# Four edits at the ends of a 2D-FFT filter stage in a mixer kernel: order of a scale, an fp32 operand, copies between SBUF tiles, late weight splits

## The chip, the cores and the metric

The kernel runs on one core of one Trainium2 chip. The metric is the device time of one execution in microseconds (us). The time before is 972.05 us, the median of three runs that lie between 971.56 and 975.56 us.

## The reference

Two blocks A (a spectral filter) and B (a token MLP) alternate, twice each, on x of 2048 tokens by 640 channels:

```python
def _A_ref(x, w_r, w_i):
    X = rfft2(x)                 # over tokens and channels
    return irfft2(X * (w_r + 1j * w_i), (S, D))
def _B_ref(x, w1, b1, w2, b2):
    u = gelu(einsum("bsd,sf->bdf", layernorm(x), w1) + b1)
    return (einsum("bdf,fs->bds", u, w2) + b2).transpose(0, 2, 1)
x = x + _A_ref(layernorm(x), w_r, w_i)
x = x + _B_ref(layernorm(x), w1, b1, w2, b2)
x = x + _A_ref(layernorm(x), w_r, w_i)
x = x + _B_ref(layernorm(x), w1, b1, w2, b2)
```

## The kernel before

The filter block is done with matrix products against tables. Three stages of code carry it. In the first (`run` for block one, the last rows of `b1st` for block three) each of 16 token tiles is normalised, folded and multiplied by `tM`; the result goes to two tiles of fp16, the rounded value `s1h` and the remainder `s1l`, 80 columns of 128 values each: columns 0 to 63 are four classes of 16 groups, columns 64 to 79 one "rest" column for each group. Nearly every operand of the kernel is such a pair of fp16 values, and a product takes three fp16 matmuls.

The second stage is `a1`, called the filter stage here. It runs twice, in block one (about 60 to 121 us) and in block three (about 533 to 600 us). It goes over 16 groups g of frequencies. For each group there are these steps, in the names that the order string `STEPS` gives them:

- `d` (`dstage`): the products of `s1h`, `s1l` with the table `tD`, into a PSUM slot. Groups 0 and 1 read the rest column in place; groups from 2 on read it from a stacked tile `stk`, in which the parts of one group's rest column lie under each other on partitions 0 to 31, 32 to 63 and 64 to 95. `stack(g)` fills it for two groups at a time (three buffers).
- `ph`, `pl` (`psplit`): ScalarE writes the rounded value of that PSUM slot, scaled, to fp16, and VectorE the remainder. For group 0 this is written out ahead of the order string, in two halves q.
- `sA`, `sB` (`s2half`): two half products with the table `tS2`, each in four quarters of the array (64 rows by 64 columns), three fp16 terms each, 12 matmuls of 321 columns. The two halves add into the same banks, so each `sB` waits for an instruction that itself waited for `sA`. For group 0 this instruction is a small VectorE copy on a tile called `between`.
- `ta`, `tb` (`term`): VectorE multiplies with the filter `w` and its scale `sx`. `sa`, `sb`: GpSimd adds and subtracts the terms. `xh`, `xl` split the sum (ScalarE, GpSimd), `uh`, `ul` copy a strip (ScalarE).
- `i` (`is2mm`): the product with `tI2`. `Yh`, `Yl`: its split into the tile Y (ScalarE, VectorE).

`STEPS` holds one order for each of the two calls, and each engine runs its part of it in that order (`self.pin = True`). `d1@1` means group 1 in PSUM slot 1, `ph2&1` that this instruction stands between `sA1` and `sB1`. In the first call further steps beginning with `e` are mixed in: `ep8 ev8 ep9 ev9 ev10` are the pieces of `scale_x`, which works out the scale `sx` of the filter from the sums of squares `xq`, on TensorE (p) and VectorE (v), by way of a PSUM tile (slot 1); its last piece `ev10` gives `cxe`, which scales the input of the third stage. `ea4` to `ea7` are ScalarE's part of the split of a weight tile for block two (`wsplit` with `lo=False`, into `wh`), `ev4` the scale for it.

The rest columns go from `s1h`, `s1l` to DRAM tiles `rest` (`keep`, on SyncE's queue) and from there to `stk`, in `stack`: three DMAs for the three parts and two small ones for a single row. For groups 2 and 3 (`G0`) the parts from `s1h` are issued by GpSimd, all others by SyncE. GpSimd's memset of `between` comes after `stack(G0)` in the program. DMAs issued before the order string are placed by the scheduler of the framework.

The third stage is `a2`, over 16 token tiles i: `id_mm(i)` (16 matmuls with `tDi`), `ehigh` on ScalarE (`eh`, needs `cxe`), `elow` on VectorE (`el`), then `is1_mm` (6 matmuls with `tIM`) one tile later, then sums and statistics. VectorE's part of the split of that weight tile is in the loop, at tiles 1, 2, 4 and 5. The MLP blocks `b1st` and `b2nd` follow.

In `run`, over i from 0 to 21, ScalarE writes `s1h` and VectorE `s1l` of tile i - 6, VectorE the fold `f` of tile i - 4, and ScalarE sums the squares of one filter group per step (`scan_x`).

Of the kernel before, what the change touches and what calls it, by code (L numbers as in the profile page):

```python
# [11 lines left out]
F32 = mybir.dt.float32  # L12
# [15 lines left out]
    d1@1 ep8 ph1 sA0@0 ev8 pl1 sB0 ep9 sA1@1 ev9 d2@2 tb0 d3@3 ta0 ph2&1 pl2 sb0 sB1 sa0 ea1 sA2@2 tb1 ph3 d4@0 xh0&2  # L28
# [10 lines left out]
    Yh14 Yl12 xl15b i15a@0 uh15 ul15 Yl14 i15b@3 Yh15a Yh15b Yl15a Yl15b ev4 ev10 ea4 ea5 ea6 ea7  # L39
# [9 lines left out]
    sB14 pl15 sa13 i9@1 xh12 ta14 ul10 sb13 uh12 i8@3 Yh7 tb14 xl12 Yh9 sb14 sA15@0 xh13 sa14 Yl9 uh13 ul12&15 xl13  # L49
    xh14 sB15 Yl7 ul11 i10@1 uh14 Yh8 ta15a xl14 i11@2 tb15a Yh10 ta15b ul13 sa15a tb15b ul14 Yl8 Yh11 i13@0 sb15a  # L50
# [9 lines left out]
TS = 4096.0  # L60
# [30 lines left out]
class Layers:  # L91
# [226 lines left out]
    def a0_open(self, first=False):  # L318
# [5 lines left out]
        self.tS2 = p.tile([128, 2, 2, 4, 128], F16, name=f"tS2{self.n}")  # L324
        self.tI2 = p.tile([128, 2, 2, 2, 128], F16, name=f"tI2{self.n}")
        p = self.pT = self.push("a0", side=self.sp)
# [9 lines left out]
    def a0_load(self):  # L336
        nc, A = self.nc, self.A
        nc.sync.dma_start(self.tD, A["tD"])
        nc.sync.dma_start(self.tS2, A["tS2"])
        nc.sync.dma_start(self.tI2, A["tI2"])  # L340

# [126 lines left out]
    def a1(self, first):  # L468
# [35 lines left out]

        CL = [(1, 0, 0, 160, 96), (0, 0, 160, 321, 98), (3, 1, 0, 160, 96), (2, 1, 160, 321, 96)]
# [3 lines left out]
        def stack(g):  # L509
# [4 lines left out]
            r, c = rest[g > G0], slice(g - 4, g - 4 + NC) if g > G0 else slice(0, NC)  # L514
            for k, a in ((0, 0), (1, 1), (2, 0)):
                e = nc.gpsimd if g == G0 and not a else nc.sync
                e.dma_start(q[32 * k:32 * k + 32], r[a][:, :, c].rearrange("c i g r -> i c g r"))
                if k < 2:
                    e.dma_start(q[96 + k:97 + k, 0], r[k][2, 31:32, c])

        rest = [[self.dram.tile([4, 32, n, 128], F16, name=f"rest{i}_{n}_{self.n}") for i in range(2)] for n in (NC, NG - 4)]
        def keep(i, c):

            for q, s1 in zip(rest[i], (self.s1h, self.s1l)):
                nc.sync.dma_start(q.rearrange("c i g r -> (c i) g r"), s1[:, c].rearrange("p g h a b -> p g (h a b)"))

        keep(0, slice(66, 68))
        stack(G0)
        keep(1, slice(68, 80))
# [1654 lines left out]
```

## Time and profile before

| what | us |
|---|---|
| median of three runs | 972.05 |
| the profiled execution, whole | 976.39 |
| its span, first to last instruction | 974.6 |
| filter stage of block one, first to last matmul of its order | about 60.8 to 120.3 |
| filter stage of block three | about 533.2 to 597.7 |
| granted TensorE clock, mean | 0.995 |

A row of the timeline gives the start in us from the beginning of the span, the duration, the engine, the line, the operation, output and inputs by the program's names with their shape, the number of instructions merged into the row, and in brackets how long the engine sat idle before it and what released it. A row of the windows gives the length of a stretch, the busy time and number of instructions of PE (matmuls), PEld (weight loads), VectorE (DVE), ScalarE (ACT) and GpSimd (POOL), the granted TensorE clock as a share of full speed, the share of the DMA engines that was busy, and GB/s. SPq is SyncE's queue, on which DMAs are issued. Nearly all instructions carry line 83, that of a helper, so rows are told apart by their tiles.

### The profile page before, as it was taken

To read this page: it belongs to the slowest core of one execution; us is meant where nothing else is said; L and a number is where in the kernel's file an instruction comes from. 1 tells how busy PE (TensorE), PEld (TensorE's weight loads), DVE (VectorE), ACT (ScalarE), POOL (GpSimd) and SP (SyncE) were. 2 spreads that over 40 slices of the span, in tenths; PEclk is the share of its full clock that TensorE was granted. 3 is DMA by queue.
4 is the path that set the end of the run, shared out by engine and by line. 5 is a ranking of instruction groups with operands and counts; after the bars stand their busy time and mean duration, and the time that the engine had idled before them with its cause. 6 is when DMAs were issued, how large, how long until landed. Compare 5 with 4: busy or idle time off the path is not lost.

```text
span 974.6 us, 22438 instructions
## 1 busy us (share of the span) xinstructions
PE 933.2 (96%) x8993; PEld 694.1 (71%) x8993; DVE 752.1 (77%) x1403; ACT 564.8 (58%) x868; POOL 296.2 (30%) x498
## 2 busy tenths in 40 slices
PE   4889899999999999999999898999999999999998
PEld 3778777677777777777777676776777777777776
DVE  7979989999788966566677697889645445998885
ACT  5857869895767775455544476784433335455431
POOL 6949858311111112222223595771000000000000
PEclk9999999999999999999999899999999999999999
DMA  7956367654876776654232663765555448655411
GB/s 243 303 152 172 113 230 241 230 173 159 316 279 229 274 278 202 230 170 130 93 103 92 172 184 105 246 221 161 170 156 169 144 130 287 206 189 179 134 58 43
DMA packets 68252, 179.49 MB, mean 184 GB/s; under 512 B 8026, under 2 KB 15476, under 8 KB 68148
## 3 DMA queue, kind: packets, MB, share of 16 engines
q1 hardware_dynamic: 60964, 151.70, 48.4%
q0 software_dynamic: 7184, 26.36, 7.3%
q8 instruction: 70, 1.15, 0.5%
q14 instruction: 34, 0.28, 0.1%
HBM read 130.45 MB, written 47.58 MB: 183 GB/s over the span
## 4 chain that ended last, share of the span: by engine, by line
PE 61%; DVE 16%; ACT 7%; POOL 6%; issue 4%; DMA 4%; SPq 1%; ACTq 0%; POOLq 0%; DVEq 0%
PE ps L83 61%; DVE f L83 3%; DVE st L83 3%; DVE wl L83 3%; POOL eo L83 2%; DVE s1l L83 2%; DMA xt<-x 2%; ACT wh L83 1%; DVE xt L83 1%; DVE Yl L83 1%; ACT z L83 1%; DMA raw<-w 1%; ACT junk L83 1%; POOL xl L83 1%; POOL ta L83 1%
## 5 line engine op out<-in xcount | busy, mean ns | idle before, releaser
L83 PEld LDWEIGHTS <-wh 128*128 128x128 f16 x2298 | 222.5, 98 | 88.1 <-DVE wh L83 1.6
L83 PE MATMUL ps<-u,wh 128*128 128x320 f16 x1242 | 228.6, 299 | 0.1
L83 PEld LDWEIGHTS <-wl 128*128 128x128 f16 x1626 | 158.8, 98 | 64.4 <-DVE wl L83 1.5
L83 PE MATMUL ps<-u,wl 128*128 128x320 f16 x826 | 182.1, 299 | 0.6 <-DVE v L83 0.3
L83 PEld LDWEIGHTS <-wo 128*128 128x128 f16 x924 | 90.3, 98 | 35.1
L83 POOL TENSOR_TENSOR r<-v,mh 128x1 f32<-128x1 f32 x64 | 39.5, 617 | 143.4 <-DVE nm L83 133.3
L83 PE MATMUL ps<-tDi,Yh 128*128 128x322 f16 x320 | 71.3, 300 | 1.5 <-ACT Yh L83 1.5
L83 DVE TENSOR_TENSOR f<-eo 128x256 f32<-128x256 f32 (+1 forms) x124 | 39.0, 367 | 36.5 <-POOL eo L83 35.8
L83 ACT ACTIVATE junk<-raw 128x896 bf16<-128x896 f32 (+1 forms) x60 | 59.5, 991 | 13.0 <-DMA raw<-w 12.2
L83 POOL TENSOR_TENSOR xt<-xt,ec 128x320 f32<-128x320 f32 x64 | 53.3, 853 | 29.8 <-DVE xt L83 29.7
L83 DVE BATCH_NORM_STATS2 st<-xt 128x6 f32<-128x320 f32 x126 | 55.2, 480 | 5.9 <-DMA xt<-x 5.4
L83 PE MATMUL ps<-tM,f 128*128 128x128 f32 x160 | 40.4, 434 | 19.6 <-DMA xt<-x 12.3
L83 ACT ACTIVATE z<-xt,nb,r 128x640 f32<-128x640 f32 x31 | 28.5, 919 | 52.7 <-POOL z L83 43.1
L83 PE MATMUL ps<-u,wo 128*128 128x320 f16 x420 | 58.8, 299 | 0.0
L83 POOL TENSOR_TENSOR eo<-z 128x320 f32<-128x320 f32 x60 | 52.2, 891 | 17.2 <-ACT z L83 15.2
L83 PE MATMUL ps<-tDi,Yl 128*128 128x322 f16 x192 | 55.7, 299 | 1.4 <-DVE Yl L83 1.4
L83 DVE SCALAR_TENSOR_TENSOR wl<-raw,s,wh 128x896 f16<-128x896 f32 (+2 forms) x43 | 47.9, 1123 | 7.4 <-ACT wh L83 7.4
L83 PEld LDWEIGHTS ps<-tM,f 128*128 128x128 f32 x160 | 35.1, 315 | 24.7 <-DVE f L83 24.3
L83 POOL TENSOR_TENSOR xl<-ta,xh 128x642 f16<-128x642 f32 (+2 forms) x34 | 45.5, 1345 | 7.9 <-ACT xh L83 7.8
L83 DVE SCALAR_TENSOR_TENSOR u<-f,su,u 128x1280 f16<-128x1280 f32 (+2 forms) x26 | 25.5, 996 | 25.9 <-ACT u L83 25.8
L83 POOL MEMSET wl<- 64x256 f16 x2 | 0.6, 306 | 146.7 <-DMA wl<-w2A 144.3
L83 ACT ACTIVATE wh<-raw,s 128x896 f16<-128x896 f32 (+2 forms) x46 | 43.5, 987 | 2.1 <-DVE s L83 1.8
(255 smaller groups left out, 2239.4 us busy)
## 6 DMA issues: line engine op xcount, KB each, us to landing
xt<-x SPq DMA_DIRECT2D x79, 320.0 KB
raw<-w SPq DMA_DIRECT2D x32, 512.0 KB
w<-w SPq DMA_DIRECT2D x48, 321.0 KB
x<-xt SPq DMA_DIRECT2D x47, 320.0 KB
raw<-w SPq DMA_DIRECT2D x32, 448.0 KB
raw<-w2z SPq DMA_DIRECT2D x32, 448.0 KB
out<-xt SPq DMA_DIRECT2D x15, 320.0 KB
w1S<-wl POOLq DMA_DIRECT2D x9, 512.0 KB, 6.2
```

The lines of the kernel that those rows point to most:

```text
L83: i = f(*a, **k)
```

## The change

- In the first call's order `ep8 ev8` come ahead of `d1`, `ep9 ev9` ahead of `ph1`, `sB0` ahead of `pl1`; the scale's PSUM tile is slot 3. At the end `ev10` comes ahead of `ev4`.
- Group 0's P is one fp32 tile written by two ScalarE instructions; `sA0` and `sB0` are four fp32 matmuls each with a new fp32 table `tS1`. Group 0's part of `tS2` is dropped.
- `stack(2)` copies straight from `s1h`, `s1l` to `stk`, in 12 DMAs of 32 partitions (512 bytes each) and two of one row; the DRAM tiles for groups 2 and 3 go.
- The memset of `between` is ahead of all of these DMAs.
- `ea4` to `ea7` move into the loop of `a2`, one after `ehigh` of each of tiles 0 to 3.
- In the second call's order, near the end, `sB15` stands behind `xh13` in place of `ul12`, and `Yl7`, `Yh9` change places with their neighbours.
- In `run`, `s1l` of tile 12 comes after the fold of tile 15, and the last four sums of squares come two by two.

```diff
-    d1@1 ep8 ph1 sA0@0 ev8 pl1 sB0 ep9 sA1@1 ev9 d2@2 tb0 d3@3 ta0 ph2&1 pl2 sb0 sB1 sa0 ea1 sA2@2 tb1 ph3 d4@0 xh0&2
+    ep8 ev8 d1@1 ep9 ev9 ph1 sA0@0 sB0 pl1 tb0 sA1@1 d2@2 ta0 d3@3 ph2&1 pl2 sb0 sB1 sa0 ea1 sA2@2 tb1 ph3 d4@0 xh0&2
...
-    Yh14 Yl12 xl15b i15a@0 uh15 ul15 Yl14 i15b@3 Yh15a Yh15b Yl15a Yl15b ev4 ev10 ea4 ea5 ea6 ea7
+    Yh14 Yl12 xl15b i15a@0 uh15 ul15 Yl14 i15b@3 Yh15a Yh15b Yl15a Yl15b ev10 ev4
...
-    sB14 pl15 sa13 i9@1 xh12 ta14 ul10 sb13 uh12 i8@3 Yh7 tb14 xl12 Yh9 sb14 sA15@0 xh13 sa14 Yl9 uh13 ul12&15 xl13
-    xh14 sB15 Yl7 ul11 i10@1 uh14 Yh8 ta15a xl14 i11@2 tb15a Yh10 ta15b ul13 sa15a tb15b ul14 Yl8 Yh11 i13@0 sb15a
+    sB14 pl15 sa13 i9@1 xh12 ta14 ul10 sb13 uh12 i8@3 Yh7 tb14 Yl7 xl12 sA15@0 xh13&15 Yh9 sb14 uh13 sa14 Yl9 ul12 xl13
+    xh14 sB15 ul11 i10@1 uh14 Yh8 ta15a xl14 i11@2 tb15a Yh10 ta15b ul13 sa15a tb15b ul14 Yl8 Yh11 i13@0 sb15a
...
+        between = p.tile([128, 2], F32, name=f"between{self.n}")
+        G.memset(between, 0.0)
...
+            if g == G0:
+                for k, s1, e in ((0, self.s1h, nc.sync), (2, self.s1h, nc.gpsimd), (1, self.s1l, nc.sync)):
+                    part = s1[:, 64 + g:64 + g + NC].rearrange("p g h a b -> p g (h a b)")
+                    for c in range(4):
+                        e.dma_start(q[32 * k:32 * k + 32, c], part[32 * c:32 * c + 32])
+                    if k < 2:
+                        e.dma_start(q[96 + k:97 + k, 0], part[95:96])
+                return
...
+            if g == 0:
+                for R, C in ((0, 0), (0, 1), (1, 1), (1, 0)):
+                    ri, q = R ^ half, R ^ C
+                    out.append(mm(
+                        ps[HALF[C], ri, :NL], self.tS1[HALF[R], 2 * ri + q, HALF[C]], x[HALF[R], q, :NL],
+                        start=half == 0, stop=half == 1,
+                    ))
+                return out[0], out[-1]
...
-        pp[0] = tuple(self.t(p, [128, 2, 322], F16, a, 3) for a in ("ph", "pl"))
-        sc = PQS / (S1S * TS)
+        pp[0] = p.tile([128, 2, 322], F32, name=f"pf{self.n}")
         for q in range(2):
-            a, b, c = ps[:, q, :NL], pp[0][0][:, q, :NL], pp[0][1][:, q, :NL]
-            T.activation(b, a, AF.Copy, scale=sc)
-            V.scalar_tensor_tensor(c, a, sc, b, op0=ALU.mult, op1=ALU.subtract)
+            T.activation(pp[0][:, q, :NL], ps[:, q, :NL], AF.Copy, scale=PQS / (S1S * TS))
...
-                    made["x"] = self.scale_x(p, slots[1])
+                    made["x"] = self.scale_x(p, slots[3])
...
                 eo[i] = ehigh(pd[i])
+                if first and i < 4:
+                    c = i ^ 2
+                    self.wsplit(0, (c // 2,), lo=False, part=slice(c % 2 * 4, c % 2 * 4 + 4))
...
-            if has[6]:
-                self.a0_s1l(i - 6, pv.pop(i - 6), 1.0)
+            for k in () if i == 18 else (i - 7, i - 6) if i == 19 else (i - 6,):
+                if 0 <= k < NJ:
+                    self.a0_s1l(k, pv.pop(k), 1.0)
...
-            if i >= 6 and scans:
-                scans.pop(0)()
+            for _ in range(2 if i in (18, 19) else 1):
+                if i >= 6 and scans:
+                    scans.pop(0)()
```

More of the change, by code (lines that the diff above doesn't have):

```diff
@@ L340, in a0_load @@
         nc.sync.dma_start(self.tI2, A["tI2"])
+        nc.sync.dma_start(self.tS1, A["tS1"])
     CA, CB = 1.0 / ZS ** 2, EPS / ZS ** 2
@@ L513, in stack @@
             q = stk[g] = self.t(p, [128, 4, NC, 128], F16, "stk", NSTK)
[L514 removed]
+            if g == G0:
[6 more added lines that the diff above has]
+                return
+            c = slice(g - 4, g - 4 + NC)
             for k, a in ((0, 0), (1, 1), (2, 0)):
[L516 to L517 removed]
+                nc.sync.dma_start(q[32 * k:32 * k + 32], rest[a][:, :, c].rearrange("c i g r -> i c g r"))
                 if k < 2:
[L519 to L527, printed above, removed]
+                    nc.sync.dma_start(q[96 + k:97 + k, 0], rest[k][2, 31:32, c])
+        rest = [self.dram.tile([4, 32, NG - 4, 128], F16, name=f"rest{i}_{self.n}") for i in range(2)]
         stack(G0)
[L529 removed]
+        for q, s1 in zip(rest, (self.s1h, self.s1l)):
+            nc.sync.dma_start(q.rearrange("c i g r -> (c i) g r"), s1[:, 68:80].rearrange("p g h a b -> p g (h a b)"))
         def wload(g):
@@ L650, in a1 @@
         dst, half, home = {}, {}, {}
-        between = p.tile([128, 2], F32, name=f"between{self.n}")
-        G.memset(between, 0.0)
         tt = collections.defaultdict(dict)
```

8 lines of the change are left out of this document (5 added, 3 removed).

## The prediction

> **What bounds the kernel now.** I read the page's head first, its chain of work that ended last, then the windows of 25 us.
>
> ```profile
> PE 933.2 (96%) x8993; PEld 694.1 (71%) x8993; DVE 752.1 (77%) x1403; ACT 564.8 (58%) x868; POOL 296.2 (30%) x498
> ...
> PE 61%; DVE 16%; ACT 7%; POOL 6%; issue 4%; DMA 4%; SPq 1%; ACTq 0%; POOLq 0%; DVEq 0%
> ...
> 50.00:75.00 25.00, 21.96 (x353) 18.07 (x354) 19.53 (x42) 12.78 (x27) 10.55 (x20) 0.93 0.56 161
> ...
> 525.00:550.00 25.00, 20.17 (x334) 16.05 (x336) 15.73 (x34) 7.32 (x13) 7.76 (x12) 0.86 0.45 136
> 550.00:575.00 25.00, 24.43 (x648) 19.99 (x644) 24.42 (x36) 17.38 (x35) 23.19 (x27) 1.00 0.64 184
> ...
> 700.00:725.00 25.00, 25.00 (x186) 18.01 (x185) 9.06 (x15) 8.29 (x12) 0.00 (x0) 1.00 0.52 157
> ```
>
> TensorE is busy 96% of the span and holds 61% of the chain, so there is little to win outside its idle places and its slow places. Both filter stages begin with one: of all windows only 50 to 75 and 525 to 550 have a clock below 1.00 (third number from the end), with 21.96 and 20.17 us of TensorE work. Once a stage runs (550 to 575), TensorE, VectorE and GpSimd are all busy over 92%: it then goes at its own pace, and a start that comes earlier by some us moves all that follows. In the MLP behind it TensorE has no gap at all (700 to 725), so I let such a shift through whole.
>
> The start of the second filter stage, from the timeline and two windows (length, TensorE work, and the clock third from the end):
>
> ```profile
> 533.34 0.80 SPq L525 DMA_DIRECT2D rest<-s1h  x2
> 535.21 0.44 ACT L83 ACTIVATE ph<-ps 128x321 f16<-128x321 f32 x1 [1.90 <-PE ps L83]
> 536.57 0.24 PE L83 MATMUL ps<-tD,s1l 128*64 128x161 f16 x2
> 537.24 0.33 PE L83 MATMUL ps<-ph,tS 64*64 64x321 f16 x4 [0.43 <-DVE pl L83]
> 537.37 0.33 PE L83 MATMUL ps<-pl,tS 64*64 64x321 f16 x4
> 537.72 0.64 POOL L517 DMA_DIRECT2D stk<-rest  x1 [6.87 <-issue]
> 539.41 0.12 POOL L83 MEMSET between<- 128x2 f32 x1
> 539.77 0.33 PE L83 MATMUL ps<-ph,tS 64*64 64x321 f16 x4 [1.93 <-DVE between L83]
> 542.96 0.34 PE L83 MATMUL ps<-tD,stk 96*64 96x160 f16 x2 [1.13 <-issue]
> 546.99 0.48 PE L83 MATMUL ps<-ph,tS 64*64 64x321 f16 x4
> 547.95 0.89 DVE L83 SCALAR_TENSOR_TENSOR tb<-ps,sx,w 128x642 f32<-128x642 f32 x1 [1.43 <-PE ps L83]
> 548.23 0.33 PE L83 MATMUL ps<-tD,s1h 128*64 128x160 f16 x4
> 549.49 0.33 PE L83 MATMUL ps<-ph,tS 64*64 64x321 f16 x4
> ...
> 537.50:540.90 3.40, 1.34 (x36) 0.66 (x27) 1.33 (x3) 0.05 (x1) 1.81 (x4) 0.99 0.87 264
> 540.90:547.60 6.70, 5.57 (x84) 4.59 (x80) 2.04 (x3) 1.16 (x2) 1.46 (x2) 0.50 0.56 152
> ```
>
> Three losses stand in line. sB0 (539.77) waits 1.93 us for VectorE's copy of `between`, which waits for GpSimd's memset, which is queued behind GpSimd's three DMAs, which wait for `rest` to land in DRAM. Group 2's first stacked product (542.96) waits 1.13 us for those DMAs. And after 3.4 us with only 1.34 us of matmuls the clock is granted at 0.50 for 6.7 us. From tb1 (547.95) on the stage is at its pace.
>
> **The price of an fp32 half product** comes first, as `sA0` and `sB0` stand in both starts. No row shows an fp32 matmul of a quarter of the array.
>
> ```profile
> 531.38 1.35 PE L83 MATMUL ps<-mr,ft 128*128 128x128 f32 x10 [0.29 <-ACT mr L83]
> ```
>
> One fp32 matmul of the program is two instructions, and ten of 128 columns took 1.35 us, 0.135 each. The fp16 quarters of 321 columns begin 0.13 to 0.14 us apart by fours (537.24, 537.37): four run side by side, and a half of three terms takes 0.41 us. An fp32 instruction of 321 columns lies between 0.27 us (two fp16 passes) and 0.34 us (0.135 × 321 / 128). I take 0.28. A half has eight of them: 0.56 us if the quarters run side by side as fp16's do; 8 × 0.28 = 2.24 if none overlaps. Between: if the two of one quarter follow each other and matmuls begin in program order, the second of a quarter overlaps only the first of the next, 5 × 0.28 = 1.4 us. I take **1.4**, since order of starts is what every merged row of TensorE shows, and keep both ends. The Trainium skill (TensorE: Matmul & The Clock Gate, "The mechanism") says that matmuls start and end strictly in program order while different tiles of the array overlap; by it 1.4 stands and the sum is 967.2; 0.56 (964.1) is out. The fp16 rows agree with both, and no run here shows it for fp32.
>
> **Start of the second stage.** P: the two ScalarE copies of 0.44 us end at 536.1, before group 1's `d` is streamed (536.57 + 0.13 = 536.7), so P no longer holds TensorE and its two VectorE remainders are gone. sA0 536.75 to 538.15. Then the copy of `between`, its memset long done, with the bare gap that stage one shows (0.52 us, next fence): sB0 538.67 to 540.07. sA1 0.41, `d2` and `d3` 1.26 each (548.23 to 549.49), at full clock: 543.0. sB1 to 543.4, tb1 at 543.6 against 547.95: **4.35 us earlier**. It needs two things. The stacked tile must be there by 540.7: GpSimd's four DMAs can be issued when `s1h` is done, where SyncE now sends it to `rest`, at 533.34; at the 0.64 us of the row they end at 535.9, and from the end of the old issues (539.41) to use were 3.5 us, so 539.4. SyncE issues ten DMAs from 533.34 on (the last five are from `s1l`), at 0.40 us each (two in 0.80) up to 537.4, and the last must land in 3.3 us. And the clock must stay: TensorE now is idle 0.5 us in place of 2.5, so I let it.
>
> The Trainium skill (same page, "What's actually happening") puts the drop to half clock down to an idle window of about 3.4 us. The gaps here are 0.43 and 1.93 us, with sA0 between, so the trace drops earlier than that sentence has it; the rival below takes it up.
>
> **Start of the first stage**, from the timeline:
>
> ```profile
> 60.75 0.33 SPq L525 DMA_DIRECT2D rest<-s1h  x1
> 64.12 0.23 PE L83 MATMUL ps<-tD,s1l 128*64 128x161 f16 x2
> 64.29 0.39 PE L83 MATMUL ps<-eye,xq 128*16 128x128 f32 x2
> 64.78 0.33 PE L83 MATMUL ps<-ph,tS 64*64 64x321 f16 x4
> 65.71 0.33 PE L83 MATMUL ps<-ph,tS 64*64 64x321 f16 x4 [0.32 <-DVE between L83]
> 66.88 0.39 PE L83 MATMUL ps<-eye,xb 16*128 16x16 f32 x2 [0.56 <-DVE pl L83]
> 67.20 0.33 PE L83 MATMUL ps<-ph,tS 64*64 64x321 f16 x4
> 68.14 0.26 PE L83 MATMUL ps<-tD,stk 96*64 96x160 f16 x2
> ...
> 68.69 0.89 DVE L83 SCALAR_TENSOR_TENSOR tb<-ps,sx,w 128x642 f32<-128x642 f32 x1
> ```
>
> Here `between` is in time: sA0 streams 64.78 to 65.19, sB0 starts at 65.71, the gap of 0.52. The scale's second matmul (66.88) waits for pl1 because it writes the slot that pl1 reads, and sA1 stands behind it. All that goes: ep8 (two instructions, 0.27) and ep9 (short) now lie ahead, their VectorE pieces beside `d1`. So `d1` ends near 64.45, sA0 64.55 to 65.95, sB0 66.47 to 67.87, sA1 at 67.87 against 67.20. tb0 comes a little earlier (68.1 against 68.69), but tb1 depends on `d2`, `d3` and sB1 behind sA1: the stage starts **0.65 us later**. The fp32 halves cost 2 × 1.0 us, and what they free (P's remainders, the waits of 0.32 and 0.56, the scale) is 1.35. The stack is needed at 68.8 in place of 68.14, and its first DMAs can be issued at 60.75, where `s1h` now goes to `rest`: 8 us ahead.
>
> **End of the first stage**, from the timeline of ScalarE and TensorE:
>
> ```profile
> 122.67 2.56 ACT L83 ACTIVATE wh<-raw,s 128x512 f16<-128x512 f32 x4 [1.77 <-DVE s L83]
> ...
> 125.66 0.30 PE L83 MATMUL ps<-tDi,Yl 128*128 128x322 f16 x1
> 126.89 0.41 PE L83 MATMUL ps<-el,tIM 128*128 128x322 f32 x1 [0.51 <-DVE el L83]
> 127.75 0.45 PE L83 MATMUL ps<-tDi,Yh 128*128 128x322 f16 x2
> 129.81 0.30 PE L83 MATMUL ps<-tDi,Yl 128*128 128x322 f16 x1
> 130.84 0.45 PE L83 MATMUL ps<-tDi,Yh 128*128 128x322 f16 x2
> ```
>
> Four weight splits hold ScalarE to 125.2, then come `eh` of tile 0 and `el`. TensorE's step from the last `id_mm` product to the next takes 2.09 us (125.66 to 127.75) against 1.03 in the next round (129.81 to 130.84). An `id_mm` takes 2.1 us (127.75 to 129.81 and its last step), so `id_mm(0)` ended 2.1 us before `id_mm(1)`, at 123.7. With `ev10` first and the splits behind it, `eh` can start there and not at 125.2 (122.67 + 2.56): 1.5 us, more than the 1.05 that is lost. **1.05 us earlier**. The splits now stand in ScalarE's queue ahead of the next tile's `ec`; at 0.64 us each in rounds of 3.1 us they find room, and VectorE's part of a split comes one tile later as before.
>
> **The rest.** At the second stage's end sB15 waits 1.71 us for a ScalarE copy:
>
> ```profile
> 590.07 0.33 PE L83 MATMUL ps<-ph,tS 64*64 64x321 f16 x4 [1.71 <-ACT xl L83]
> ...
> 590.45 2.79 POOL L83 TENSOR_TENSOR xl<-ta,xh 128x642 f16<-128x642 f32 x2
> 593.20 0.63 POOL L83 TENSOR_TENSOR ta<-ta,tb 128x256 f32<-128x256 f32 x1
> ```
>
> That wait falls to about 0.5, but group 15's sums (593.20) follow GpSimd's `xl`, which end then whatever sB15 does: 0.1 us, 1.2 at the most. The order in `run` I put at nothing: TensorE's last products there are what the filter waits for, and their folds of tiles 14 and 15 are in time; if a late filter load held ScalarE's doubled sums, some tenths.
>
> **Sum.** −4.35 + 0.65 − 1.05 − 0.1 = −4.85 us. The profiled execution took 976.39 us, 4.3 above the median; I take the sum from the median: 972.05 − 4.85 = **967.2**. The bounds of the fp32 half give 2 × 0.84 us either way at each start: at 2.24 both starts lose 1.7, 970.6; at 0.56 the first gains 1.7, the second at most 1.4 before the stack binds (it lands near 539.4), 964.1.
>
> **Rivals.**
>
> 1. The quarters run side by side: 964.1. For it: fp16's do. Against: two instructions per quarter, in order. Chance 0.2.
> 2. No overlap of fp32 quarters: 970.6. For it: no row shows any. Chance 0.17.
> 3. The clock falls in spite of it, for a reason other than the gap of 1.93 us: then 4.6 us of matmuls (542.96 to 547.6) run at half, 2.3 us lost, 969.5. By the skill's rule on the idle window this is the case; the row of 1.34 us in 3.4 speaks for the gaps. Chance 0.07.
> 4. **Slower**: fourteen small DMAs in place of five are late. Each us that the stack lands after 540.7 (second stage) or 68.8 (first) is lost in each stage; when TensorE is idle some 2 us, the half clock is back (2.3 us). With L us of lateness in both, 2L + 2.3 must be over 4.85: it decides from L = 1.3 on, and at L = 3 the time is 975.5. For it: SyncE's queue now has ten issues ahead of `rest` for groups 4 on, the filter loads behind them, and the DMA engines are at 0.87 in 537.5 to 540.9. Against: the detour over DRAM, which made the old wait, is gone, and the margins are about 1 and 4 us. The Trainium skill (DMA: Bandwidth & Descriptors, "Rules for kernel authors") advises one transfer over all partitions rather than many small ones; the rival is what that would do here. Chance 0.08.
>
> The forecast keeps 0.48. **Range** 963.8 to 971.5: it holds the forecast, the first three rivals, and leaves out the fourth and the edges. 0.5% is 4.9 us, about what a measurement of this kernel can tell from no change; 967.2 lies on that line, so the forecast is split: faster by over 0.5% 0.2 + 0.25 = 0.45, within 0.51, slower 0.04.
>
> **What would show it.** In the changed profile: sB0 of the second stage with no wait for `between` over 0.5 us; the window 541 to 547 at clock 1.00; the rows of fp32 quarters of 64x321, whose steps give the half (1.4, or 0.56, or 2.24); tb1 at about 543.6 (less what the first stage shifts); no wait of TensorE for the stack; the step of 2.09 us at the first stage's end at 1.03. Wrong it is if the fp32 half is over 2 us, if the clock is still 0.50, or if a later filter load or the stack of groups 4 and 5 takes the place of the wait, on VectorE's `tb` or on `d4`.

## The result, and the profile after

| | before | after |
|---|---|---|
| median of the runs, us | 973.28 (971.56 to 975.56, 4 runs) | 985.78 (980.66 to 987.12, 4 runs) |
| profiled execution: time, span, us | 976.39, 974.6 | 986.96, 985.2 |

The ratio after / before is **1.0117, 95% interval 1.0072 to 1.0162**: by the ratio some 11 us slower, where 4.85 us faster was forecast. The time lies above the range; it is the case of the fourth rival.

The head of the page and its chain of work that ended last, for the changed kernel:

```profile
span 985.2 us, 22431 instructions
...
PE 936.5 (95%) x8977; PEld 694.0 (70%) x8977; DVE 751.0 (76%) x1399; ACT 563.8 (57%) x868; POOL 297.7 (30%) x500
...
PE 57%; DVE 15%; ACT 7%; POOL 5%; issue 5%; DMA 3%; SPq 1%; ACTq 0%; DVEq 0%; POOLq 0%
```

The windows of 25 us over the same places (length, busy time of TensorE, its weight loads, VectorE, ScalarE, GpSimd, then clock, DMA share, GB/s):

```profile
50.00:75.00 25.00, 19.34 (x284) 15.26 (x286) 17.04 (x37) 11.10 (x24) 10.82 (x19) 0.90 0.47 138
525.00:550.00 25.00, 20.69 (x312) 15.28 (x310) 14.50 (x35) 8.15 (x14) 8.62 (x15) 1.00 0.33 107
550.00:575.00 25.00, 21.89 (x514) 17.76 (x516) 20.30 (x29) 13.09 (x25) 17.81 (x20) 0.86 0.61 177
...
600.00:625.00 25.00, 23.06 (x308) 18.26 (x303) 17.63 (x38) 12.49 (x24) 10.45 (x21) 0.88 0.23 71
700.00:725.00 25.00, 25.00 (x186) 18.01 (x185) 15.10 (x22) 10.32 (x14) 0.00 (x0) 1.00 0.54 163
```

TensorE's work is the same (936.5 us against 933.2), so the 10.6 us of span are waits and slow stretches. The second start has its clock at 1.00 in 525 to 550, as forecast, but the low clock has moved behind it: 0.86 in 550 to 575, where the kernel before ran at 1.00 with 24.43 us of matmuls. The first start has lost 2.6 us of matmuls (19.34 for 21.96), and its DMA engines were less busy than before (0.47 for 0.56).

SyncE's queue at the first start of the changed kernel, from the timeline (start, length, line, DMA):

```profile
59.78 2.49 SPq L522 DMA_DIRECT2D stk<-s1h  x4
62.70 1.07 SPq L524 DMA_DIRECT2D stk<-s1h  x1
63.88 2.43 SPq L522 DMA_DIRECT2D stk<-s1l  x4
66.35 0.70 SPq L524 DMA_DIRECT2D stk<-s1l  x1
67.10 0.58 SPq L535 DMA_DIRECT2D rest<-s1h  x1
67.72 0.43 SPq L535 DMA_DIRECT2D rest<-s1l  x1
...
71.51 0.78 SPq L528 DMA_DIRECT2D stk<-rest  x2
...
537.18 3.66 SPq L522 DMA_DIRECT2D stk<-s1h  x4
540.88 0.59 SPq L524 DMA_DIRECT2D stk<-s1h  x1
541.52 2.49 SPq L522 DMA_DIRECT2D stk<-s1l  x4
544.05 0.59 SPq L524 DMA_DIRECT2D stk<-s1l  x1
```

And TensorE's waits there, from its timeline, with the two windows behind the second and the fourth of them:

```profile
68.41 0.26 PE L83 MATMUL ps<-tD,stk 98*64 98x161 f16 x2 [1.26 <-DMA stk<-s1l]
...
73.69 0.34 PE L83 MATMUL ps<-tD,stk 96*64 96x160 f16 x2 [1.85 <-DMA stk<-rest]
...
546.05 0.26 PE L83 MATMUL ps<-tD,stk 98*64 98x161 f16 x2 [1.57 <-DMA stk<-s1l]
...
552.99 0.35 PE L83 MATMUL ps<-tD,stk 96*64 96x160 f16 x2 [3.51 <-DMA stk<-rest]
```

```profile
73.70:77.20 3.50, 3.50 (x51) 2.56 (x52) 0.55 (x1) 0.71 (x1) 1.55 (x3) 0.53 0.68 181
...
552.90:558.00 5.10, 5.01 (x72) 3.98 (x74) 2.79 (x5) 1.02 (x2) 1.46 (x2) 0.50 0.61 155
```

In each stage ten small copies take SyncE's queue 7.3 to 7.5 us (59.78 to 67.05, 537.18 to 544.64). The DMA engines are nearly idle meanwhile, and full behind it, when the writes to `rest`, the stacks and two filter loads go out together (the share is the last number but one):

```profile
537.20:544.60 7.40, 6.29 (x138) 4.57 (x134) 4.70 (x8) 1.48 (x3) 2.22 (x5) 1.00 0.13 27
546.00:550.00 4.00, 3.43 (x80) 2.68 (x80) 0.83 (x1) 2.16 (x3) 0.00 (x0) 1.00 1.00 343
```

So the issues, not the bandwidth, set the pace of the copies. TensorE waits twice: first for the last copies of `s1l`, then for the stack of groups 4 and 5, whose round trip over DRAM can begin only behind the ten. The chain of waits says the second in two rows:

```profile
545.31 3.28 DMA rest<-s1l
...
549.33 3.52 DMA stk<-rest
```

The longer wait of each stage is followed by half clock. The loss of the two starts can be added up on TensorE's timeline. First start: waits 1.26 + 1.85, and 3.5 us at 0.53, which is 1.6 more, 4.7 in all. Second start: 1.57 + 3.51, and 5.1 us at 0.50, 2.5 more, 7.6 in all. Of these 12.3 us the other edits take back some: from 63.9 to 78.1 us the trace loses 3.8 us net, from 533.2 to 556.3 us 2.9 (table below). The rest of its 11.0 us arises elsewhere: 1.8 us between 130.8 and 176 us, and 4.2 us between 556 and 607 us. Part of that is half clock behind waits which the kernel before has too, without half clock: 0.79 us for `el` at 175.46 (0.80 before, at 173.11) and 1.21 us for `Yl` at 609.42 (the same before, at 600.12).

### The profile page after: what moved, and what is told of

Read it like the earlier page. It is cut to its first block, busy times and chain, and to the rows that moved or that the text cites. A ratio compares the mean times of both kernels' runs of the same rounds, so it can differ in the third digit from the quotient of the medians.

```text
span 985.2 us, 22431 instructions
## 1 busy us (share of the span) xinstructions
PE 936.5 (95%) x8977; PEld 694.0 (70%) x8977; DVE 751.0 (76%) x1399; ACT 563.8 (57%) x868; POOL 297.7 (30%) x500
## 3 DMA queue, kind: packets, MB, share of 16 engines
q8 instruction: 70, 1.15, 0.5%
## 4 chain that ended last, share of the span: by engine, by line
PE 57%; DVE 15%; ACT 7%; POOL 5%; issue 5%; DMA 3%; SPq 1%; ACTq 0%; DVEq 0%; POOLq 0%
PE ps L83 57%; DVE wl L83 3%; POOL eo L83 2%; DVE f L83 2%; DVE st L83 2%; DVE xt L83 1%; ACT z L83 1%; ACT wh L83 1%; DVE Yl L83 1%; DMA xt<-x 1%; ACT junk L83 1%; DVE s1l L83 1%; POOL xt L83 1%; ACT xt L83 1%; POOL ta L83 1%
## 5 line engine op out<-in xcount | busy, mean ns | idle before, releaser
L83 PE MATMUL ps<-tM,f 128*128 128x128 f32 x160 | 37.1, 402 | 21.3 <-DMA xt<-x 12.0
L83 PEld LDWEIGHTS ps<-tM,f 128*128 128x128 f32 x160 | 31.6, 284 | 26.5 <-DVE f L83 26.0
```

Of the source, the lines that this page charges most:

```text
L83: i = f(*a, **k)
```

## The experiments

A trace is one profiled execution (a look, in the expectations). To compare traces, I aligned the sequence of TensorE's matmuls with that of the kernel before. The table gives the start of the same product less its start before, in us, at products that stood before at: 63.9 (in group 1's `d`), 78.1 (first stage running), 130.8 (behind its end), 533.2 (second stage begins), 556.3 (running), 606.7 (behind its end), 965.0. The last columns are the median and the ratio to the kernel before, from 4 to 12 timed executions of each (for the ratios, 20 to 34 of the kernel before; 4 for the change). e4 is the kernel before with 27 DMAs behind its last output; it was run once, and its time holds them.

| kernel | 63.9 | 78.1 | 130.8 | 533.2 | 556.3 | 606.7 | 965.0 | median | ratio, 95% interval |
|---|---|---|---|---|---|---|---|---|---|
| the change | -0.5 | +3.3 | +2.2 | +3.8 | +6.8 | +11.0 | +11.0 | 985.78 | 1.0117, 1.0072 to 1.0162 |
| e1_via_dram | -0.2 | -1.4 | -2.5 | +0.1 | -3.9 | -1.2 | -0.4 | 975.8 | 1.001, 0.9991 to 1.0029 |
| e2_copies_only | 0.0 | +3.9 | +4.2 | +3.1 | +5.1 | +4.7 | +4.5 | 984.53 | 1.0084, 1.0057 to 1.0112 |
| e3_copies_spread | -0.4 | +0.1 | -0.9 | +0.1 | -1.8 | +0.2 | 0.0 | 977.46 | 1.0016, 0.9995 to 1.0037 |
| e4_dma_battery | -0.1 | +0.2 | +0.4 | +0.6 | -2.8 | -2.9 | -2.6 | 990.26 | none |
| e5_rest_on_act | +0.1 | +0.4 | -0.7 | -0.4 | -1.9 | -0.1 | -0.1 | 977.07 | 1.0024, 1.0011 to 1.0037 |
| e6_end1_undone | -0.3 | -1.5 | -0.9 | -0.8 | -4.8 | -0.6 | -0.1 | 975.29 | 1.0006, 0.999 to 1.0022 |
| e7_steps2_undone | -0.5 | -1.7 | -2.7 | -2.9 | -7.1 | -5.2 | -5.0 | 973.85 | 0.999, 0.9975 to 1.0004 |
| e8_fp16_p | 0.0 | -0.8 | -1.1 | -0.5 | -2.4 | +0.2 | +0.2 | 974.41 | 0.9995, 0.9979 to 1.0012 |
| f1_no_fp32_no_order | -0.7 | -1.5 | -2.5 | -2.3 | -2.7 | -2.6 | -2.7 | 973.81 | 0.9991, 0.9977 to 1.0004 |
| f2_between_only | -0.6 | +0.2 | +0.4 | +0.8 | 0.0 | +0.1 | +0.3 | 974.95 | 0.9994, 0.9984 to 1.0005 |
| f3_order_only | -0.8 | -0.7 | -0.5 | -0.1 | -0.4 | -0.8 | -0.8 | 975.59 | 0.9999, 0.9984 to 1.0014 |
| f6_rest_first | -0.3 | +1.6 | +0.6 | +2.1 | +2.0 | +2.9 | +3.0 | 981.35 | 1.0059, 1.0041 to 1.0077 |
| f7_s1l_copies | +0.7 | -0.1 | -1.0 | -1.1 | -5.7 | -5.9 | -6.0 | 971.81 | 0.9963, 0.9949 to 0.9978 |

One kernel's executions spread over 3 to 9 us, so a trace shows where time goes, and the ratio how much stays.

### Are the copies the cause?

**e1_via_dram**: the change with the remainders of groups 2 and 3 through DRAM as before, and an order that keeps stack(4) behind stack(2) in SyncE's queue.

```diff
-            if g == G0:
-                for k, s1, e in ((0, self.s1h, nc.sync), (2, self.s1h, nc.gpsimd), (1, self.s1l, nc.sync)):
...
+            with self.after(*prior):
+                for k, a in ((0, 0), (1, 1), (2, 0)):
+                    e = nc.gpsimd if g == G0 and not a else nc.sync
+                    e.dma_start(q[32 * k:32 * k + 32], r[a][:, :, c].rearrange("c i g r -> i c g r"))
```

> The change with one part undone: groups 2 and 3 get their remainders by way of DRAM again, the parts from s1h issued by GpSimd, all other edits kept. Theory I (the ten small copies hold SyncE's queue at about 0.6 us each, so that the stack of groups 2 and 3 and, behind them, the DRAM copy for groups 4 on come late): no wait of TensorE for the stack of groups 4 and 5 (1.85 and 3.51 us in the changed kernel), at most 1.2 us for that of groups 2 and 3, and 966 to 971 us, below the kernel before. Theory II (the other edits, such as the fp32 half products or the new order, do the harm): it stays near 984 us.

**e2_copies_only**: the kernel before, with the changed kernel's `stack` and its copies alone.

```diff
+                for k, s1, e in ((0, self.s1h, nc.sync), (2, self.s1h, nc.gpsimd), (1, self.s1l, nc.sync)):
...
+                        e.dma_start(q[32 * k:32 * k + 32, c], part[32 * c:32 * c + 32])
```

> The kernel before with the copies between SBUF tiles alone. Theory I: SyncE's copies take about 0.6 us each, TensorE waits for the stack of groups 4 and 5 by over 1.5 us in both stages, and the time is 8 to 14 us above the kernel before. Theory II: within 3 us of it.

**e3_copies_spread**: the change with the writes to `rest` first (`keep`, by SyncE), and the copies on three queues.

```diff
+        keep(0)
+        keep(1)
+        copies(G0, 0, self.s1h, nc.scalar)
+        copies(G0, 2, self.s1h, nc.gpsimd)
+        copies(G0, 1, self.s1l, nc.sync)
```

> The changed kernel with the same 14 copies, but spread: the first five from ScalarE's queue, four from GpSimd's as before, five from SyncE's, and SyncE issues the DRAM copies for groups 4 on ahead of its five. Theory I (the time on the issuing queue): SyncE is done some 3 us earlier, the wait for groups 4 and 5 is gone, that for groups 2 and 3 under 0.7 us, 965 to 973 us, though ScalarE's own five may delay P by up to 2 us. Theory III (a copy between SBUF tiles is slow under way, whoever issues it): the waits stay, 980 us or more.

Without the copies the loss is gone (ratio 1.001), though the 966 to 971 us that the first theory gave are missed. The copies alone, with none of the other edits, cost 0.84%, 8.2 us of 975 (the trace, of the fastest of the five executions, shows 4.5 of them). Spread over three queues, and behind the writes to `rest`, they cost next to nothing over e1 (1.0016). TensorE's timeline of the kernel with the copies alone has the waits of the change:

```profile
74.34 0.34 PE L83 MATMUL ps<-tD,stk 96*64 96x160 f16 x2 [2.24 <-DMA stk<-rest]
...
545.08 0.34 PE L83 MATMUL ps<-tD,stk 98*64 98x161 f16 x2 [1.37 <-DMA stk<-s1l]
...
552.33 0.35 PE L83 MATMUL ps<-tD,stk 96*64 96x160 f16 x2 [2.40 <-DMA stk<-rest]
```

So it is the copies, and of them the queue that they stand in. e3 missed its 965 to 973 us: waits of 0.77 and 1.40 us for the stack of groups 4 and 5 remain, and it has a price of its own. ScalarE's five issues stand ahead of its copies of P, and TensorE waits 0.64 and 2.03 us for `pf`.

### What does one such DMA cost its queue?

**e4_dma_battery**: the kernel before, with 27 DMAs issued by SyncE one after the other behind its last output (4 each of small copies from SBUF to SBUF, to DRAM and back, and three larger ones). It adds work at the end and changes nothing ahead of it.

```diff
+            for c in range(4):
+                e.dma_start(b[32:64, c], a[:32])
+            for c in range(4):
+                e.dma_start(b[:, c], a)
...
```

> The kernel before with a row of DMAs on SyncE's queue behind its last output, in sets: four copies of 32 partitions by 512 bytes from SBUF to SBUF, four of 128 partitions, four of one row, four of 32 partitions from SBUF to DRAM, four from DRAM to SBUF, four of one row from DRAM, two of 32 partitions by 2048 bytes from DRAM. Theory I, first form (a copy between two SBUF tiles is slow to issue by itself): the SBUF to SBUF sets take about 0.6 us for each, the others 0.3. Second form (the issue is slow only while the queues are full of other traffic): all take about 0.3 here. The total is 20 to 40 us above the kernel before.

SyncE's timeline; L1902 copies 32 partitions of 512 B within SBUF, L1904 all 128, L1906 one row, L1908 writes 32 partitions of 512 B to DRAM, L1909 128 of 2048 B, L1911 reads 32 of 512 B back, L1913 one row:

```profile
969.25 2.53 SPq L1902 DMA_DIRECT2D batb<-bata  x4
971.88 2.48 SPq L1904 DMA_DIRECT2D batb<-bata  x4
974.41 0.59 SPq L1906 DMA_DIRECT2D batb<-bata  x1
...
977.50 1.51 SPq L1908 DMA_DIRECT2D batd<-batb  x3
...
980.09 0.34 SPq L1909 DMA_DIRECT2D batd<-batb  x1
...
982.11 1.70 SPq L1911 DMA_DIRECT2D batb<-batd  x4
983.85 1.16 SPq L1913 DMA_DIRECT2D batb<-batd  x4
```

A copy within SBUF holds the queue for 0.59 to 0.63 us, whether it has one row, 32 partitions or 128; a write to DRAM takes 0.34 to 0.57, a read from DRAM 0.29 to 0.43. The forecast had 0.40 for each of the ten, from a row of two writes to DRAM. For copies within SBUF it is their number that counts, not their bytes; the writes and reads do not follow their bytes either (128 rows of 2048 B took 0.34, 32 of 512 B 0.50 to 0.57). The first form of the theory came in; the whole, 15 us above the kernel before, is less than the 20 to 40 expected.

### How do the two delays divide the loss?

**f6_rest_first**: the change with the two writes of groups 4 to 15 moved ahead of the copies.

```diff
-        stack(G0)
         for q, s1 in zip(rest, (self.s1h, self.s1l)):
...
+        stack(G0)
```

> The change with its two large writes of groups 4 to 15 issued by SyncE ahead of the copies into stack(2); nothing else moved. If the whole loss is the issue time of the copies on SyncE's queue (theory I): TensorE's wait for stk<-rest, 1.85 and 3.51 us in the changed kernel, is gone or under 0.5 in both passes; the copies of s1l end 1.0 us later (the writes' own 0.58 and 0.43 issue), so the wait for stk<-s1l grows from 1.26 and 1.57 to 2.0 to 2.8 each; the clock may still fall behind it. Net 1.5 to 5 us earlier than the changed kernel's 985.8: 980 to 984. If the two delays are one and the same (the stack's last copy decides, and the write of rest is hidden by it): the wait for stk<-rest goes, but the time stays at 984 to 987.

```profile
73.54 0.26 PE L83 MATMUL ps<-tD,stk 96*64 96x160 f16 x2 [0.29 <-DMA stk<-rest]
...
543.15 0.34 PE L83 MATMUL ps<-tD,stk 96*64 96x160 f16 x2 [1.58 <-DMA stk<-s1l]
...
544.97 0.35 PE L83 MATMUL ps<-tD,stk 98*64 98x161 f16 x2 [1.07 <-DMA stk<-s1l]
```

The wait for stk<-rest falls from 1.85 to 0.29 us in the first stage and goes in the second. The median falls by 4.4 us, from 985.78 to 981.35: within the expected 980 to 984, though the two intervals still touch (1.0072 to 1.0162, 1.0041 to 1.0077). The copies still cost 0.59%, through the stack alone (the two waits of 1.58 and 1.07 us in the second stage, and clock 0.50 from 543 to 549 us behind the first of them; in the first stage 1.23 and 1.00 us, at full clock).

### Where do the other edits' gains go?

e1 has every edit but the copies and is no faster than the kernel before, though its rows are 2.5 us ahead behind the first stage and 3.9 ahead in the second. Six kernels were built to find an edit that takes the gain back. The last two of them are the kernel before with some of the edits.

**e5_rest_on_act**: e1 with all of stack(2) on SyncE's queue, and the writes for groups 4 to 15 on ScalarE's (both of them, where the expectation names one).

```diff
-                    e = nc.gpsimd if g == G0 and not a else nc.sync
+                    e = nc.sync
...
-                nc.sync.dma_start(q.rearrange("c i g r -> (c i) g r"), s1[:, c].rearrange("p g h a b -> p g (h a b)"))
+                (nc.scalar if i else nc.sync).dma_start(q.rearrange("c i g r -> (c i) g r"), s1[:, c].rearrange("p g h a b -> p g (h a b)"))
```

> The change with the remainders through DRAM as before, all of stack(2) issued by SyncE, and the two large writes of groups 4 to 15 split: s1h's from SyncE, s1l's from ScalarE's queue. Theory G (what the other edits save at the starts and ends of the filter stages is given back behind them, by VectorE's loop and by transfers): in the look, TensorE's 1.47 us wait for the stack in the second pass falls to under 0.8, tb1 there comes 0.7 to 1.5 us earlier than the 543.5 of the kernel with DRAM remainders, and the time is 973 to 976, at most 1.5 us under that kernel's 975.8. Rival H (one of the remaining edits costs time where it was put, and the gains themselves reach the end): the earlier stack is kept up to the end, 970 to 973.5.

**e6_end1_undone**: e1 with the first stage's end as before.

```diff
-    Yh14 Yl12 xl15b i15a@0 uh15 ul15 Yl14 i15b@3 Yh15a Yh15b Yl15a Yl15b ev10 ev4
+    Yh14 Yl12 xl15b i15a@0 uh15 ul15 Yl14 i15b@3 Yh15a Yh15b Yl15a Yl15b ev4 ev10 ea4 ea5 ea6 ea7
...
-                if first and i < 4:
-                    c = i ^ 2
-                    self.wsplit(0, (c // 2,), lo=False, part=slice(c % 2 * 4, c % 2 * 4 + 4))
```

> The change with DRAM remainders and the first stage's end as before (the four copies ea4 to ea7 and ev4, ev10 back at the end of the list, out of the loop behind it). Theory G: the end of stage 1 is 1.0 to 1.1 us later than with the edit (rows aligned with the kernel before stand at -1.4 in place of -2.46 at 127 us), the waits for el at 160 and 172 us are gone or under 0.3, and from 175 us on the rows stand within 0.5 us of those with the edit (-0.9): 974.5 to 977. Rival H: the four copies inside the loop are what makes el late, so that without them -1.4 or better is kept past 175 us, and the kernel ends 0.5 to 1.5 us earlier than with them. Third possibility, the edit is worth its full 1.05 us up to the end: rows from 175 us on 0.5 us or more later than with the edit.

**e7_steps2_undone**: e1 with the second list of steps as before.

```diff
-    sB14 pl15 sa13 i9@1 xh12 ta14 ul10 sb13 uh12 i8@3 Yh7 tb14 Yl7 xl12 sA15@0 xh13&15 Yh9 sb14 uh13 sa14 Yl9 ul12 xl13
-    xh14 sB15 ul11 i10@1 uh14 Yh8 ta15a xl14 i11@2 tb15a Yh10 ta15b ul13 sa15a tb15b ul14 Yl8 Yh11 i13@0 sb15a
+    sB14 pl15 sa13 i9@1 xh12 ta14 ul10 sb13 uh12 i8@3 Yh7 tb14 xl12 Yh9 sb14 sA15@0 xh13 sa14 Yl9 uh13 ul12&15 xl13
+    xh14 sB15 Yl7 ul11 i10@1 uh14 Yh8 ta15a xl14 i11@2 tb15a Yh10 ta15b ul13 sa15a tb15b ul14 Yl8 Yh11 i13@0 sb15a
```

> The change with DRAM remainders and the second list of steps as before (sA15, xh15, sB15 and Yl7 in their old places). Theory G: rows at 597 us and at the end within 0.5 us of those with the edit (-1.2), the two waits for xh and Yl at 588 to 590 us being one of about 1.7 us for xl again: 974.5 to 977. Rival H: the new order costs time; without it the rows at 597 us stand at -2 or better, and the time is 1 to 2 us less.

**e8_fp16_p**: e1 with P of group 0 in two fp16 pieces again.

```diff
-        pp[0] = p.tile([128, 2, 322], F32, name=f"pf{self.n}")
+        pp[0] = tuple(self.t(p, [128, 2, 322], F16, a, 3) for a in ("ph", "pl"))
...
+            T.activation(b, a, AF.Copy, scale=sc)
+            V.scalar_tensor_tensor(c, a, sc, b, op0=ALU.mult, op1=ALU.subtract)
```

> The change with DRAM remainders and group 0's P in two fp16 pieces again. If fp32 P costs nothing (its quarters run side by side: 0.77 us for eight instructions, against three bursts of 0.33 that follow each other 0.14 apart for fp16 pieces, and VectorE's split of 0.4 falls away): sA1's first product comes 0.2 to 1 us later than the 66.22 with fp32, in the second pass likewise, and the end is 0 to 1 us later: 975 to 978. If it costs what the prediction had (0.65): sA1 comes 0.4 us or more earlier than with fp32, and the time is 974 to 975.5.

**f1_no_fp32_no_order**: the diffs of the last two at once. Left of the change are the early scale, the first stage's end, `between` first, and `run`; like e1, it keeps stack(4) behind stack(2) in SyncE's queue.

> The kernel before with four parts of the change alone: early scale, the first stage's end, `between` first, and the order of `run`; P in fp16, the second list of steps as before, remainders through DRAM. Theory M (the second list's new order is what takes the gain of the remaining edits back: two waits of 0.89 and 1.15 us for xh and Yl in place of one of 1.71 for xl, after which the clock falls in some programs): in the look there is one wait of about 1.7 us for xl and none for xh at the end of the second stage, rows behind it stand at -3 us or better against the kernel before, 970 to 974. Rival N (the order costs only its 0.33 us, and what the starts gain is lost to whatever comes last in each program's own run): rows at 605 us between -2 and +0.5, 973.5 to 976.

**f3_order_only**: the kernel before with the second list of steps in the new order (the lines with "-" and "+" of e7 the other way round).

> The kernel before with the second list of steps in the new order, nothing else. Theory M: up to 580 us the rows stand within 0.5 us of the kernel before; at the end of the second stage two waits (0.89 for xh, 1.15 for Yl) stand for one of 1.71 for xl, and the rows at 605 us stand at +0.3, or at +1.3 to +2.5 if the clock falls behind them; 975 to 977. Rival: the order gains what it saves ahead of sA15 and the rows at 605 us stand at -0.5 or better.

No single edit does it. e5 missed: the stack waits longer (2.73 us in the second pass), not shorter. The first stage's end is worth its 1.05 us where it stands (from 121 to 131 us e6 goes from -0.97 to -0.89, e1 from -1.40 to -2.46), but e1 gives 1.5 back by 176 us, while with the same edit e7 gives back 0.5 and f1 and f7 nothing. The second list's order looked guilty in e7, as its rival H expected (2 us in the median, 4.6 at the end of the trace, but 3.0 of these stand ahead of that list, at 533.2). Alone it changes nothing (f3: 0.9999, its rows at -0.78 ahead of that place and -0.75 behind it). e8's `sA1` begins 0.6 us later than e1's (66.86 for 66.22), as its first case has it, but its time lies in the range of the second, so the time doesn't decide. f1 fits neither of its two theories: its time lies in both ranges, its rows (-2.6) in neither. What the new order does is replace one wait by two, here from e6's timeline of TensorE:

```profile
586.14 0.33 PE L83 MATMUL ps<-ph,tS 64*64 64x321 f16 x4 [0.89 <-ACT xh L83]
...
587.90 0.40 PE L83 MATMUL ps<-tI,xh 64*128 64x128 f16 x4 [1.15 <-DVE Yl L83]
```

Behind these two the clock falls in some traces (the change, e6, e8) and not in others (e1, e3, e5, f3, f6). Some 10 us later every kernel, the one before too, waits 0.73 to 0.79 us for `Yh` and 1.21 for `Yl`; behind that the clock falls in the change, e6, e7, e8 and f6, which costs each about 1.5 us, and not in the other ten. Further waits come and go in the same way: 0.7 to 1.8 us "issue" inside a run of like products between 574 and 588 us (the change, e1, e3, e5, e6, and none of the other ten), a wait of VectorE for an `xt` load at 155 to 157 us (0.97 in e1, 0.94 in e3, 0.38 in e7). Each of the seven "issue" gaps ends 1.2 to 1.5 us behind the end of a 16 KB packet of DMA queue q8, which the page calls "instruction"; that hints at TensorE waiting for its own program, and no run tests it.

e4 tells what one execution can do by itself. Up to its last output its instructions are those of the kernel before, but for one VectorE memset at 813 us. Yet its trace loses 0.9 us between 131 and 176 us, and gains 3.4 between 533 and 556. So differences of this size between two single traces need no edit, and a gain or loss in one trace that the ratio doesn't show is not the edit's. Which of e1's gains are real, and why they don't reach its time, stays **open**.

### What sets the second stage's start?

**f2_between_only**: the kernel before with the memset of `between` ahead of the remainders, nothing else.

```diff
+        between = p.tile([128, 2], F32, name=f"between{self.n}")
+        G.memset(between, 0.0)
         CL = [(1, 0, 0, 160, 96), (0, 0, 160, 321, 98), (3, 1, 0, 160, 96), (2, 1, 160, 321, 96)]
...
-        between = p.tile([128, 2], F32, name=f"between{self.n}")
-        G.memset(between, 0.0)
```

> The kernel before with the memset of `between` moved ahead of the remainders, nothing else. If the 1.93 us wait for `between` at 539.77 us is what set the second pass's start and the half clock behind it (the prediction's step b without the copies): that wait is 0.3 us, the clock stays at 1.00 from 541 to 548 us, and tb1 comes 3 to 4 us earlier than 547.95; 971 to 975 if the rest of the stage keeps it, 974 to 976 if it is given back. If the stack sets the start whatever `between` does: the wait moves to the stack (2 to 4 us ahead of its first product), the clock falls there, and tb1 comes within 1 us of 547.95.

The second expectation came in. The wait of 1.93 us for `between` is gone, and in its place stands one for the stack, then a stretch at clock 0.50 (545 to 547 us); the row at 556 us has not moved:

```profile
538.96 0.33 PE L83 MATMUL ps<-ph,tS 64*64 64x321 f16 x4 [0.31 <-DVE between L83]
...
543.48 0.26 PE L83 MATMUL ps<-tD,stk 96*64 96x160 f16 x2 [2.85 <-DMA stk<-rest]
```

In this execution the stack binds, whatever comes ahead of it, and f1 has the same with 3.33 us. The time (0.9994) agrees. But what holds the stack is not the same in every execution. Here is e4, with the memset in its old place:

```profile
533.92 0.80 SPq L525 DMA_DIRECT2D rest<-s1h  x2
...
536.12 0.64 POOL L517 DMA_DIRECT2D stk<-rest  x1 [4.68 <-issue]
...
538.75 0.33 PE L83 MATMUL ps<-ph,tS 64*64 64x321 f16 x4 [0.33 <-DVE between L83]
...
542.13 0.26 PE L83 MATMUL ps<-tD,stk 96*64 96x160 f16 x2 [1.71 <-DMA stk<-rest]
...
540.90:547.60 6.70, 5.47 (x138) 4.50 (x138) 3.60 (x6) 2.87 (x4) 2.60 (x3) 1.00 0.56 146
```

From SyncE's first write to GpSimd's first read of `rest` it is 2.2 us here (533.92 to 536.12); in the trace before the change it was 4.4 (533.34 to 537.72). With 2.2 the memset is in time, the wait for `between` is 0.33 us, and the window of 540.9 to 547.6 us runs at clock 1.00 with 138 matmuls, where it had 84 at 0.50. The other traces in which GpSimd reads `rest` fall into the same two groups: 2.1 to 2.3 us in e1, e6, e7 and e8, 4.1 to 4.5 in f1, f2 and f3. So the same instructions have the wait for `between` and its 3.4 us in one execution and not in the other, and a late `rest` tells the two apart. Why it is late is not shown. That gives a version to try.

**f7_s1l_copies**: f1 with one remainder alone copied within SBUF, by GpSimd's queue: that of `s1l`, the later of the two. `s1h`'s goes through DRAM by SyncE.

```diff
+                    if g == G0 and a:
+                        part = self.s1l[:, 66:68].rearrange("p g h a b -> p g (h a b)")
+                        for c4 in range(4):
+                            nc.gpsimd.dma_start(q[32:64, c4], part[32 * c4:32 * c4 + 32])
+                        nc.gpsimd.dma_start(q[97:98, 0], part[95:96])
+                        continue
```

> The kernel with early scale, the first stage's end, `between` first and the order of `run` (P in fp16, second list as before), with the remainder of s1l for groups 2 and 3 copied from SBUF to SBUF by five DMAs of GpSimd's queue and that of s1h through DRAM by SyncE alone. If a copy costs its issue time on its own queue and nothing more: the s1l rows come at 5 x 0.64 us from s1l's end and about 2 us behind that, no later than the stack's s1h rows through DRAM, so that TensorE's 3.33 us wait for the stack in the second pass falls to 1 to 2.5 us; 971 to 974. If GpSimd's copies get in the way of its own work or land as late as the round trip: the wait stays at 3 us or more, 974 to 977.

```profile
533.51 2.06 POOL L525 DMA_DIRECT2D stk<-s1l  x4 [3.69 <-DVE s1l L83]
535.56 0.49 POOL L526 DMA_DIRECT2D stk<-s1l  x1
...
539.55 0.26 PE L83 MATMUL ps<-tD,stk 98*64 98x161 f16 x2 [0.23 <-DMA stk<-s1l]
```

In its timeline the copies are issued in 2.5 us on a queue that has nothing else to send at that time, the wait for the stack is 0.23 us, and the clock is 1.00 throughout the start. The second start gains 4.6 us (-1.1 to -5.7), and this time the gain holds to the end of the trace. The ratio is **0.9963, 95% interval 0.9949 to 0.9978**: faster than both kernels, by 0.4% and, by the two ratios, about 1.5%. TensorE's wait came out under the 1 to 2.5 us expected, the time within 971 to 974. It leaves out fp32 P and the second list's order; with them it wasn't tried.

## Why the prediction was wrong

- **The step that failed** stands in the start of the second stage: "SyncE issues ten DMAs from 533.34 on ..., at 0.40 us each (two in 0.80) up to 537.4, and the last must land in 3.3 us." The ten took 7.46 us in place of 4.06 (537.18 to 544.64, the start shifted by 3.84 as the whole stage is). The 0.40 was the price of a write to DRAM; a copy within SBUF takes about 0.6 by itself (e4), and so did nine of the ten, while the third took 1.82 for a reason that no run shows. The landing was not the trouble: the last copy was in use 1.4 us behind its issue (544.64 to 546.05), where 3.3 were allowed.
- **The fourth rival was right, its chance and its price were not.** It had the cause (ten issues ahead of `rest` for groups 4 on) at 0.08. Its rule decides from L = 1.3 us of lateness; the stack alone was late by 1.26 and 1.57. Left out was a second lateness behind the first: the round trip for groups 4 and 5, 1.85 and 3.51 us. f6, which removes it, gives back 4.4 us. With 1.26 + 1.57 + 1.85 + 3.51 and the half clock of 1.6 + 2.5 the rival's own sum would have been near 12 us of loss against 4.85 of gains. The advice to move one transfer over all partitions and not many small ones (the Trainium skill, DMA: Bandwidth & Descriptors, "Rules for kernel authors") agrees with e4: one copy over 128 partitions took its queue as long as one over 32.
- **Start of the second stage**, 4.35 us: not a loss of every execution. From 533 to 556 us e1 gains 4.0, e6 4.0, e7 4.2, f7 4.6, but e4 gains 3.4 with none of the edits, and f1 with `between` first 0.3. The prediction took the loss from one execution of 976.39 us and subtracted it from a median of 972.05; over 20 to 34 executions that median is 974.9 to 975.7. The reason was half right: f2 shows that the wait for `between` hid one for the stack.
- **The price of an fp32 half product** was 1.4 us and is 0.6. The two halves of the first stage begin 1.12 us apart, of which 0.52 is the gap that the prediction had:

```profile
64.08 0.77 PE L83 MATMUL ps<-pf,tS 64*64 64x321 f32 x8
65.20 0.77 PE L83 MATMUL ps<-pf,tS 64*64 64x321 f32 x8 [0.34 <-DVE between L83]
```

  The eight start as two rounds of four, at 64.08 to 64.10 us and at 64.40 to 64.42, so the four quarters run side by side in fp32 as in fp16, which was the first rival's mechanism. What failed is the step that the two instructions of one quarter follow each other. By the Trainium skill's rule of strict order (TensorE: Matmul & The Clock Gate, "The mechanism"), as the prediction applied it, it would be 1.4; the row decides against that reading.
- **Start of the first stage**: forecast 0.65 us later. From 63.9 to 78.1 us the kernels with fp32 P and a stack in time gain 1.2 (e1, e6, e7), those with fp16 P 0.8 (e8, f1, f7). So in these traces fp32 P is worth 0.4 us, and the early scale and the rest 0.8, give or take what a trace without them shows there (+0.1 to +0.8 in e4, f2 and f3); the sign was wrong by the mis-sized half. A slow clock was not to be won there: in the window of 50 to 75 us the clock of the kernel before is low at 56 to 60 us (0.53 and 0.62), ahead of the stage, and 1.00 from 60 us on. (A third window below 1.00, 950 to 975 with 0.99, was passed over.)
- **End of the first stage**, 1.05 us earlier: right. TensorE's step from the last product of `id_mm(1)` to the next is 1.03 us in the changed kernel:

```profile
128.95 0.30 PE L83 MATMUL ps<-tDi,Yl 128*128 128x322 f16 x1
...
129.98 0.45 PE L83 MATMUL ps<-tDi,Yh 128*128 128x322 f16 x2
```

- **The rest**: the second stage's end came out at nothing when alone (f3), against 0.1 forecast. The wait of 1.71 us became two, 0.89 and 1.15, and not 0.5.
- **That a shift goes through whole** held between 556 and 607 us for f1, f7 and e4, not for e1, e6 and e8. There 2.6 to 4.2 us went (1.8 to 1.9 in e3, e5 and e7), as 4.2 did in the changed kernel's own trace.

## What to carry to other kernels

Price a moved DMA by a row of its own kind (same source, same destination), multiply by the number of issues, and then write down what that queue sends next and who needs it: here the second transfer in line cost about as much as the first. Before a wait is priced, see in a second trace of the same kernel whether it is there again. To shorten a detour over DRAM, copy only the piece that arrives last, on a queue that has nothing else to send. And when a wait is removed, look for the one that it hid before counting it as a gain.

## What the hardware showed that was not expected

- A DMA from SBUF to SBUF holds SyncE's queue for about 0.6 us, one row or 128 partitions alike; a read of one row from DRAM holds it for 0.29 (e4). On GpSimd's queue a copy took 0.5 to 0.56 us (2.06 for four in f7, 2.23 in the change). Single issues take much longer now and then (1.82 us for one copy in the change, 2.01 for one write to `rest` before).
- The way of `rest` through DRAM, from the first write's issue to the first read's, took 2.1 to 2.3 us in five traces and 4.1 to 4.5 in four, and both in the same kernel (e4, and the kernel before).
- The length of a wait alone doesn't tell whether the clock falls. It fell to about half behind single waits of 1.37 (e2), 1.58 (f6), 1.85, 2.06, 2.24, 2.40, 2.73, 2.85, 3.33 and 3.51 us at the starts, not behind 1.28, 1.40, 1.42, 1.47, 1.71 (e4) and 2.03 (e3). Behind two waits of 0.89 and 1.15 it fell in three traces of eight. The Trainium skill (TensorE: Matmul & The Clock Gate, "What's actually happening") speaks of an idle window of about 3.4 us; here the clock fell behind single waits of half that and less. The same section calls the window free-running; by that the same gaps can end on either side, as they did in e6 and e1, but no run here shows the window itself.
- Eight fp32 instructions of 321 columns on four quarters of the array took 0.77 us from the first start to the last end; an fp16 half of twelve instructions took 0.61 before the change (64.78 to 65.39).
